# Block-causal attention and a gated feed-forward layer on one core: the constant of unseen keys is added by one-row products on PE instead of by ACT, the planner's ranks are set anew, and the last tokens' second half gets a tile of its own

## The chip, the core and the metric

The kernel runs on one core of a Trainium2 chip. The core has five engines that run side by side, each through its own list of instructions in order: the matrix engine TensorE (PE; its weight loads are listed apart as PEld), VectorE (DVE), ScalarE (ACT), GpSimd (POOL), and SyncE (SP), which here only issues DMAs. They wait for each other through semaphores. PE reads its operands from SBUF and writes to PSUM; DVE and ACT read and write both. The metric is the time of one execution in microseconds (us), as the median of several runs.

## The reference

Inputs are `q`, `k`, `v` of 8 batches, 8 heads, 576 tokens and 64 numbers a head, and three weights of a feed-forward layer. What is computed:

```python
scores = scale * np.matmul(q, k.transpose(0, 1, 3, 2))
block_i = pos[:, None] // 64
block_j = pos[None, :] // 64
scores = np.where(block_i >= block_j, scores, -1000000000.0)
scores = scores - np.max(scores, axis=-1, keepdims=True)
attn = np.exp(scores)
attn = attn / (np.sum(attn, axis=-1, keepdims=True) + 1e-09)
x = np.matmul(attn, v)          # then heads side by side: 4608 tokens of 512
g = x @ w_gate
out = (g * (1.0 / (1.0 + np.exp(-g))) * (x @ w_val)) @ w_out
```

The feed-forward layer has 512 inputs, 1536 hidden channels and 512 outputs. A query sees the keys of its own block of 64 and of earlier ones.

## The kernel before, in words

**Attention.** The heads are worked on in pairs. Scores are laid out with 128 keys (a *chunk*) on the partitions and the queries along the rows, so 576 keys make five chunks, of which a query only needs those up to its own. In a *mixed* chunk, the one that holds a query's own block, the first 64 queries must not see the last 64 keys. There the kernel adds -1e9, which the later exponential turns into 0.

Batches 0 and 1 (`plain_scores`) are split into two stretches of queries, 0 to 256 and 256 to 576 (`FIRST`). A pair's steps are: loads of q and k; PE turns them (L403) and ACT copies them out of PSUM as `parts` (L411); PE multiplies keys by queries (L429), the two heads of a pair on 64 rows of the array each; ACT copies the scores to SBUF (`sc`, L447); ACT goes over the first 64 queries of each mixed chunk again and adds the bias `unseen` (0 for 64 keys, -1e9 for 64) with L452, and for chunk 0 also writes the start of the running maximum `mx` in two pieces (L460, and L461 with the bias). In batch 0's first stretch the scores stay in PSUM: ACT adds the bias there (L470) and copies them to `mx` (L473). Then DVE takes the maximum over the chunks (L603), POOL over the 128 keys (L607), DVE subtracts it (L631), ACT takes the exponential (L635), and PE multiplies by `v`, with the two heads on 64 columns of the array each, and for batch 0 also by `ones` for the sums (L675). Batches 2 to 7 (`split_scores`, L555 and after) work on all 576 queries of two pairs at once; their products are on the full array, and their scores, masked at L575, are not part of the change.

**Feed-forward.** Tokens come in 18 tiles of 256. Each number is split into a high and a low part, and each product is three matrix products (L998 to L1000 into `gv`, L1089 to L1091 into `po` or `at`). The weights arrive in 36 pieces (`weight`), each loaded raw into a `wo` tile and then unpacked by ACT (L857, L861, L876, with a tile `ob` that POOL has filled with zeros at L274) and by DVE (L866, L871, L879). Tiles 0 and 1 are worked on while batches 0 and 1 are, and while the weights come in.

**The order.** Each step is a task with an engine, a cost, a rank and what it waits for. `in_order` runs the program on paper with these costs and gives every engine its list: of the tasks that could start, the one of lowest rank goes next. The order on each engine is then fixed. Ranks come from tables: `FIRST` for the pairs of the first two batches, `PIECES` and `AHEAD` for the weight pieces and the earlier loads of some, `SIDE` and `MIXED` for tiles 0 and 1, `LEAD` for the later batches. Costs come from `act_us`, `dve_us`, `mm_us` and `pair_us`; PE pays 0.2 where a task's `mode` differs from the one before.

**The end.** The last 128 tokens go out in two halves, the first copied from PSUM by ACT (L1116), the second by DVE (L1114), both into one tile `ob`.

Of the kernel before, what the change touches and what calls it, by code (L numbers as in the profile page):

```python
# [18 lines left out]
def kernel(  # L19
# [33 lines left out]
    LEAD, EAGER = 1.88, 0.3  # L53
# [3 lines left out]
    MIXED = (0, 0, 0, 1, 1, 0, 1, 0, 1, 0, 1, 1)  # L57
# [3 lines left out]
    AHEAD = {(0, 1): 2.01, (0, 2): 2.03, (1, 0): 2.5, (1, 1): 2.07, (1, 2): 2.07}  # L61
    LATER = 0.6

    PIECES = [
        (2.64, 2.64, 2.71),
        (2.85, 3.37, 2.76),
        (5.12, 5.12, 4.37),
        (4.66, 4.68, 4.68),
        (2.95, 3.91, 4.11),
        (4.18, 4.18, 4.91),  # L70
        (4.71, 4.38, 4.79),
        (2.20, 2.82, 2.82),
        (1.32, 1.14, 0.01),
        (1.91, 1.85, 2.33),
        (0.26, 1.61, 0.56),
        (2.08, 2.78, 1.84),
    ]

    SIDE = (3.40, 10.26)
# [4 lines left out]
        0: [(0, 256, (2.02, 2.21, 2.06, 2.08)), (256, 576, (1.99, 2.09, 0.10, 2.03))],  # L84
        1: [(0, 256, (1.33, 2.46, 3.26, 3.40)), (256, 576, (1.79, 1.87, 2.05, 2.09))],
# [76 lines left out]
    def act_us(n):  # L162
        return 0.08 + n * 0.000833
# [19 lines left out]
    ones = const.tile([P, D], F32, name="ones")  # L183
# [4 lines left out]
    nc.vector.memset(unseen[BLK:P], HIDDEN)  # L188
    seen = const.tile([P, 1], F32, name="seen")
# [144 lines left out]
    def attention(R, b, h, a, e, early, bufs, lane):  # L334
# [4 lines left out]
        Q = R - (0.001 if early else EAGER)  # L339
# [30 lines left out]
        def plain_scores():  # L370
# [21 lines left out]
            for i in range(2):  # L392
                ps = Buf("gv") if whole else Buf("at", also=banks)
                nb = len(blocks[i])
                per = nb if nb < 6 else 3

                def turned(ps=ps):
                    return ps[0].rearrange("p (x n) -> p x n", x=1) if whole else ps[0]

                def transposes(i=i, turned=turned, per=per):  # L400
                    for m, c in enumerate(blocks[i]):
                        o = m % per * TB
                        nc.tensor.transpose(  # L403
                            turned()[:, m // per, o : o + TB],
                            qk[0][:TB, lane * 3 + c, 2 * i * D : 2 * (i + 1) * D],
                            ident[:TB, :TB],
                        )

                def out_of_psum(i=i, turned=turned, nb=nb, per=per):
                    o = L + blocks[i][0] * TB  # L410
                    nc.scalar.mul(  # L411
                        prt[i][:, o : o + nb * TB].rearrange("p (x n) -> p x n", x=nb // per),
                        turned()[:, 0 : nb // per, 0 : per * TB],
                        1.0 if i else SCALE,
                    )

                tr = add("PE", 0.083 * nb, R, transposes, [ld[i]], [qk, ps, prt])
                ready.append(add("ACT", act_us(nb * TB), R, out_of_psum, [tr], [ps, prt]))

            for visit in visits:  # L420
                both = [Buf("at", also=banks) for _ in visit]

                def products(visit=visit, both=both):
                    for parts, ps in zip(visit, both):
                        o = 0
                        for c, qs, w in parts:
                            for x in range(2):
                                rows = slice(x * D, (x + 1) * D)
                                nc.tensor.matmul(  # L429
                                    ps[0][:, x, o : o + w],  # L430
                                    lhsT=prt[1][rows, L + c * P : L + (c + 1) * P],
                                    rhs=prt[0][rows, L + qs : L + qs + w],
                                    start=True,
                                    stop=True,
                                )
                            o += w

                ws = [w for parts in visit for _, _, w in parts]
                pr = add("PE", pair_us(*ws), Q, products, ready, [*both, prt, sc], mode="rows")
                for parts, ps in zip(visit, both):  # L440
                    gw = sum(w for _, _, w in parts)
                    mixed = [(c, sum(w for _, _, w in parts[:i])) for i, (c, qs, _) in enumerate(parts) if qs == c * P]
# [6 lines left out]
                    def hide(mixed=mixed, ps=ps):  # L449

                        for c, o in mixed:
                            nc.scalar.activation(  # L452
                                sc[0][:, :, place[c] : place[c] + BLK],
                                ps[0][:, :, o : o + BLK],
                                AF.Identity,
                                bias=unseen,
                            )

                    def first_max(ps=ps):
                        nc.scalar.copy(mx[0][:, :, L + BLK : L + P], ps[0][:, :, BLK:P])  # L460
                        nc.scalar.activation(  # L461
                            mx[0][:, :, L : L + BLK], ps[0][:, :, 0:BLK], AF.Identity, bias=unseen
                        )

                    if whole:
                        stays.append(ps)

                        def hide_there(ps=ps):
                            x = ps[0].rearrange("p x (n w) -> p x n w", w=2 * P)[:, :, :, 0:BLK]
                            nc.scalar.activation(x, x, AF.Identity, bias=unseen)  # L470

                        def max_there(ps=ps):
                            nc.scalar.copy(mx[0][:, :, L : L + W], ps[0][:, :, 0:W])  # L473

                        t = add("ACT", act_us(4 * BLK) + 0.1, Q, hide_there, [pr], [ps])
                        t = add("ACT", act_us(2 * W), Q, max_there, [t], [ps, mx])
# [3 lines left out]
                    t = add("ACT", act_us(2 * gw), Q, out_of_psum, [pr], [ps, sc])  # L480
                    if mixed:
                        t = add("ACT", 0.28 * len(mixed), Q, hide, [t], [ps, sc])
                    if parts[0][:2] == (0, 0):
                        t = add("ACT", 0.46, Q, first_max, [t], [ps, mx])
# [3 lines left out]
        def split_scores():  # L488
# [48 lines left out]
            for x in range(2):  # L537
                for group in (((0, 0, half), (0, half, half)), ((1, 4), (2, 3))):
# [42 lines left out]
                    t = add("ACT", act_us(2 * gw), Q, out_of_psum, [pr], [ps, sc])  # L581
# [105 lines left out]
        for i, s0, s1, _ in pieces:  # L687
# [4 lines left out]
            if s1 - s0 > here:  # L692
                ends.append(add("ACT", act_us(s1 - s0 - here), R, out_of_psum, [pr], [ps, xu]))

        if here:
# [15 lines left out]
            t = add("DVE", 1.2, 1.0, invert, [pr], [ps, sr, xt])  # L711
# [54 lines left out]
        if direct:  # L766
# [4 lines left out]
            sm = [add("ACT", act_us(W - here), R, sums_there, [pr], [ps, sr])] * 2  # L771
# [40 lines left out]
    def weight(i, kind):  # L812
# [70 lines left out]
        if wide:  # L883
            t = add("ACT", act_us(DM), R, signs, [t], [raw, y])
            f = add("DVE", dve_us(DM), R, fraction, [t], [raw, y], True)
            t = add("ACT", act_us(DM), R, scaled, [t], [raw])
            t = add("DVE", dve_us(DM), R, exponent, [t, f], [raw], True)
        t = w_high[i, kind] = add("ACT", act_us(DM), R, high, [t], bufs)
# [75 lines left out]
    def feed_forward(j, t0, w, xs):  # L964
# [50 lines left out]
        for i in range(0, NFC, 2):  # L1015
# [35 lines left out]
            a = add("ACT", act_us(n), E, tanh, [tg], [pg, t])  # L1051
# [53 lines left out]
        for m in range(nb):  # L1105
            ob = Buf("ob", "out")

            halves = 2 if ends_alone and m == nb - 1 else 1
            for x in range(halves):
                cols = slice(x * DM // halves, (x + 1) * DM // halves)  # L1110
# [11 lines left out]
                us = (dve_us if x else act_us)(DM // halves)  # L1122
# [61 lines left out]
    def in_order():  # L1184
# [17 lines left out]
        spare = {"PE": 2.0, "DVE": 0.3, "ACT": 0.3, "POOL": 0.0, "SP": 0.0}  # L1202
# [107 lines left out]
```

## Time and profile before

| | us |
|---|---|
| median of 3 runs | 1183.08 (1180.5 to 1184.99) |
| the profiled execution | 1180.03 |
| its span, first to last instruction | 1178.2 |
| PE busy | 1148.2 (97%) |
| DVE busy | 768.9 (65%) |
| ACT busy | 635.9 (54%) |
| POOL busy | 324.9 (28%) |
| 16 DMA engines, share in q1 | 56.8% |

The profile is of one execution. An engine is busy while an instruction of its own runs; waits, branches and the issuing of DMAs don't count. Matrix products overlap, so the start of one to the start of the next says more of PE's pace than the duration of one. A product of 32-bit floats (L403 aside, all products of attention in batches 0 and 1) shows as two records, one for each pass. A name like ACTq is the engine's sequencer, where DMAs are issued. In a row of waits stands who waited, for whom, the total in us, how often, and the longest. A row of groups has the line, engine, operation, tiles and shapes, the count, then the busy time and the mean in ns, then idle time before and what ended it. Buffer numbers are left out of tile names.

### The profile page before, as it was taken

What the parts mean: (1) busy time and instruction counts of PE and PEld (TensorE: products, weight loads), DVE (VectorE), ACT (ScalarE), POOL (GpSimd) and SP (SyncE); (2) the same over time, 40 slices, a digit from 0 to 9 for tenths busy, and PEclk for the clock granted to TensorE, in tenths of its full rate; (3) what the DMA queues carried; (4) which work ended last, traced back from release to release, by engine and by line L of the source; (5) the groups of instructions that cost most, each with busy time, mean ns of one, the idle gap of its engine ahead of it and who ended that gap; (6) DMA issues with size and microseconds to landing.
All of it is one profiled execution on the core that took longest, in us unless ns stands there. A gap on an engine that the chain in (4) does not pass through costs nothing.

```text
span 1178.2 us, 21734 instructions
## 1 busy us (share of the span) xinstructions
PE 1148.2 (97%) x8464; PEld 1029.9 (87%) x8464; DVE 768.9 (65%) x1234; ACT 635.9 (54%) x1150; POOL 324.9 (28%) x138
## 2 busy tenths in 40 slices
PE   6889999999999999999999999999999999999998
PEld 4667777889898989898998999898989899999997
DVE  5998988876687667877585767675767633323222
ACT  6898967757574736574655556564746312212111
POOL 3122110143634162345233325243344300000000
PEclk9999999999999999999999999999999999999999
DMA  8778656755564746755656464646662445453432
GB/s 214 188 199 214 192 180 197 208 178 160 147 169 115 210 146 176 204 164 153 181 168 182 138 192 134 198 134 190 159 199 92 153 157 183 150 167 136 144 130 103
DMA packets 266983, 197.40 MB, mean 168 GB/s; under 512 B 195264, under 2 KB 231376, under 8 KB 266880
## 3 DMA queue, kind: packets, MB, share of 16 engines
q1 hardware_dynamic: 264304, 195.29, 56.8%
q8 instruction: 66, 1.08, 0.4%
q10 hardware_dynamic: 2576, 0.72, 0.3%
q14 instruction: 37, 0.30, 0.1%
HBM read 171.57 MB, written 24.38 MB: 166 GB/s over the span
## 4 chain that ended last, share of the span: by engine, by line
PE 84%; ACT 6%; DVE 5%; DMA 2%; POOL 1%; issue 1%; SPq 0%; ACTq 0%; DVEq 0%; POOLq 0%
PE gv L998 15%; PE gv L1000 15%; PE gv L999 15%; PE po L1089 7%; PE po L1090 7%; PE po L1091 7%; PE at L555 7%; PE at L675 7%; POOL mx L607 1%; DVE mx L603 1%; DVE sc L631 1%; ACT sc L447 1%; ACT ob L857 1%; ACT sc L635 1%; DVE wo L866 1%
## 5 line engine op out<-in xcount | busy, mean ns | idle before, releaser
L607 POOL PARTITION_ALL_REDUCE mx<-mx x80 | 144.6, 1855 | 405.7 <-DVE mx L603 192.6
L998 PE MATMUL gv<-xhl,v_all 128*128 128x256 f32 x864 | 241.5, 280 | 0.7 <-DVE t L1039 0.7
L1000 PE MATMUL gv<-xhl,v_all 128*128 128x256 f32 x864 | 239.4, 277 | 0.0
L999 PE MATMUL gv<-xhl,v_all 128*128 128x256 f32 x864 | 239.3, 277 | 0.0
L726 POOL PARTITION_ALL_REDUCE mx<-mx x48 | 178.1, 3758 | 205.8 <-DVE mx L603 205.8
L1034 DVE SCALAR_TENSOR_TENSOR t<-t,gv 128x512 f32<-128x512 f32 x108 | 74.0, 685 | 209.3 <-ACT t L1031 208.9
L998 PEld LDWEIGHTS gv<-xhl,v_all 128*128 128x128 f32 x864 | 162.1, 188 | 4.9 <-issue 2.7
L999 PEld LDWEIGHTS gv<-xhl,v_all 128*128 128x128 f32 x864 | 162.3, 188 | 0.9
L1000 PEld LDWEIGHTS gv<-xhl,v_all 128*128 128x128 f32 x864 | 162.2, 188 | 0.0
L1031 ACT ACTIVATE t<-gv 128x512 f32<-128x512 f32 x108 | 64.5, 598 | 169.5 <-PE gv L1000 169.4
L1089 PE MATMUL po<-wo,hhl 128*128 128x512 f32 x372 | 147.7, 397 | 0.3 <-ACT ob L1116 0.3
L1090 PE MATMUL po<-wo,hhl 128*128 128x512 f32 x372 | 145.6, 391 | 0.0
L1091 PE MATMUL po<-wo,hhl 128*128 128x512 f32 x372 | 145.1, 390 | 0.0
L1044 ACT CAST hhl<-t 128x512 fp32r<-128x512 f32 x108 | 67.2, 622 | 139.3 <-DVE t L1039 138.0
L631 DVE TENSOR_TENSOR sc<-sc,mx 128x640 f32<-128x640 f32 (+6 forms) x168 | 123.9, 773 | 18.5 <-POOL mx L607 18.3
L635 ACT ACTIVATE sc<-sc 128x1024 f32<-128x1024 f32 (+3 forms) x104 | 105.5, 1028 | 35.8 <-DVE sc L631 35.1
L998 PE MATMUL gv<-xhl,g_even 128*128 128x256 f32 x432 | 123.2, 285 | 0.1
L999 PE MATMUL gv<-xhl,g_even 128*128 128x256 f32 x432 | 122.3, 283 | 0.2 <-DVE xhl L326 0.2
L1000 PE MATMUL gv<-xhl,g_even 128*128 128x256 f32 x432 | 122.1, 283 | 0.0
L1039 DVE SCALAR_TENSOR_TENSOR t<-t,gv 128x512 f32<-128x512 f32 x108 | 73.9, 684 | 73.1 <-PE gv L1000 72.7
L998 PE MATMUL gv<-xhl,g_odd 128*128 128x256 f32 x432 | 120.7, 279 | 0.7 <-ACT g_odd L876 0.7
L1000 PE MATMUL gv<-xhl,g_odd 128*128 128x256 f32 x432 | 119.7, 277 | 0.6 <-DVE g_odd L879 0.6
(157 smaller groups left out, 2465.2 us busy)
## 6 DMA issues: line engine op xcount, KB each, us to landing
wo<-wo_d SPq DMA_DIRECT2D x200, 512.0 KB
out_dram<-ob SPq DMA_DIRECT2D x35, 256.0 KB
v<-in_v_dram SPq DMA_DIRECT2D x64, 128.0 KB
xt<-x_d SPq DMA_DIRECT2D x64, 128.0 KB
rt<-r_d SPq DMA_DIRECT2D x128, 64.0 KB
qk<-in_q_dram SPq DMA_DIRECT2D x112, 72.0 KB
qk<-in_k_dram SPq DMA_DIRECT2D x104, 72.0 KB
x_d<-xu SPq DMA_DIRECT2D x24, 288.0 KB
```

Of the source, the lines that this page charges most:

```text
L555: nc.tensor.matmul(ps[0][:, i, o : o + w], lhsT=prt[x][1][:, c * P : (c + 1) * P], rhs=m, start=not low, stop=low == 1,)
L607: nc.gpsimd.partition_all_reduce(m, m, channels=P, reduce_op=bass_isa.ReduceOp.max)
L631: nc.vector.tensor_tensor(piece(c), scores_of(c), m, ALU.subtract)
L635: nc.scalar.activation(x, x, AF.Exp)
L675: nc.tensor.matmul(ps[0][own(x), 1 - i if sums else i, q0 - s0 : s1 - s0], lhsT=ones if sums else vt[0][:, 2 * lane + c, own(x)], rhs=sc[0 ...
L726: nc.gpsimd.partition_all_reduce(m, m, channels=P, reduce_op=bass_isa.ReduceOp.add)
L998: nc.tensor.matmul(o, lhsT=hi[:, d], rhs=xhi[:, 0:w], start=first, stop=False)
L999: nc.tensor.matmul(o, lhsT=hi[:, d], rhs=xlo[:, 0:w], start=False, stop=False)
L1000: nc.tensor.matmul(o, lhsT=lo[:, d], rhs=xhi[:, 0:w], start=False, stop=last)
L1089: nc.tensor.matmul(po, lhsT=hi, rhs=whi, start=i + y == 0, stop=False)
L1090: nc.tensor.matmul(po, lhsT=hi, rhs=wlo, start=False, stop=False)
L1091: nc.tensor.matmul(po, lhsT=lo, rhs=whi, start=False, stop=i + y == NFC - 1)
```

## The change

Four things change.

- *The constant.* A new tile `shade` has 64 columns of 0 and 64 columns of 1 (the second half now serves as `ones`), and a new tile `hidden` holds -1e9. After the products of each mixed chunk in batches 0 and 1, two more products with one row each (one for each head, from partitions 0 and 64) add `shade` times `hidden` onto the first 64 queries in PSUM. The chip's instructions name their tile of the array: 64 x 128 for the score products, 32 x 128 for the new ones. ACT's steps L452, L461 and L470 of these batches go, and L460 copies all 128 queries.
- *Costs on paper.* ACT's tasks that read PSUM cost 0.05 and the others 0.093 besides the elements (before: 0.08 for all), three steps of the weights cost more, the new products 0.117 a pair; three numbers in `spare` change.
- *Ranks.* `LEAD`, `LATER`, `MIXED`, `AHEAD`, `PIECES`, `SIDE` and `FIRST` are new. In batches 0 and 1 a task of the scores now ranks 0.3 ahead of its pair's other tasks (before: 0.001).
- *The last tokens.* The second half of the last 128 tokens goes through a `t` tile, the first through `ob`.

```diff
-    LEAD, EAGER = 1.88, 0.3
+    LEAD, EAGER = 1.79, 0.3
...
-        0: [(0, 256, (2.02, 2.21, 2.06, 2.08)), (256, 576, (1.99, 2.09, 0.10, 2.03))],
+        0: [(0, 256, (-0.54, -0.36, -5.34, -0.08)), (256, 576, (-5.88, -1.74, -1.43, -0.73))],
...
-    def act_us(n):
-        return 0.08 + n * 0.000833
+    def act_us(n, psum=False, more=0.0):
+        return (0.05 if psum else 0.093) + n * 0.000833 + more
...
-    ones = const.tile([P, D], F32, name="ones")
+    shade = const.tile([P, 2 * BLK], F32, name="shade")
+    nc.vector.memset(shade[:, 0:BLK], 0.0)
+    ones = shade[:, BLK : BLK + D]
     nc.vector.memset(ones, 1.0)
...
+    hidden = const.tile([P, 1], F32, name="hidden")
+    nc.vector.memset(hidden, HIDDEN)
...
-        Q = R - (0.001 if early else EAGER)
+        Q = R - (0.3 if early else EAGER)
...
                                     start=True,
+                                    stop=qs > c * P,
+                                )
+
+                            for x in range(2) if qs == c * P else ():
+                                nc.tensor.matmul(
+                                    ps[0][:, x, o : o + BLK],
+                                    lhsT=shade[x * D : x * D + 1, :],
+                                    rhs=hidden[x * D : x * D + 1, :].to_broadcast([1, BLK]),
+                                    start=False,
                                     stop=True,
                                 )
                             o += w
 
                 ws = [w for parts in visit for _, _, w in parts]
+                ws += [BLK for parts in visit for c, qs, _ in parts if qs == c * P]
...
-                    def hide(mixed=mixed, ps=ps):
-
-                        for c, o in mixed:
-                            nc.scalar.activation(
-                                sc[0][:, :, place[c] : place[c] + BLK],
-                                ps[0][:, :, o : o + BLK],
-                                AF.Identity,
-                                bias=unseen,
-                            )
-
                     def first_max(ps=ps):
-                        nc.scalar.copy(mx[0][:, :, L + BLK : L + P], ps[0][:, :, BLK:P])
-                        nc.scalar.activation(
-                            mx[0][:, :, L : L + BLK], ps[0][:, :, 0:BLK], AF.Identity, bias=unseen
-                        )
+                        nc.scalar.copy(mx[0][:, :, L : L + P], ps[0][:, :, 0:P])
...
-                        def hide_there(ps=ps):
-                            x = ps[0].rearrange("p x (n w) -> p x n w", w=2 * P)[:, :, :, 0:BLK]
-                            nc.scalar.activation(x, x, AF.Identity, bias=unseen)
...
-            ob = Buf("ob", "out")
...
             for x in range(halves):
+                ob = Buf("t") if x else Buf("ob", "out")
...
-        spare = {"PE": 2.0, "DVE": 0.3, "ACT": 0.3, "POOL": 0.0, "SP": 0.0}
+        spare = {"PE": 2.37, "DVE": 0.40, "ACT": 0.38, "POOL": 0.0, "SP": 0.0}
```

How the order moves, at two places. First PE, where the first feed-forward products of tile 0 (`gv`, from the gate weights `g_even`) and the scores of a pair's second stretch (`at`, `po`, from `parts`) meet. Before, from the first feed-forward product on:

```order
L998 MATMUL gv_0_138<-xhl_0_78,g_even_76 128x256
L999 MATMUL gv_0_138<-xhl_1_79,g_even_76 128x256
L1000 MATMUL gv_0_138<-xhl_0_78,g_even_77 128x256
L429 MATMUL at_0_164<-parts_0_148,parts_1_149 128x320 x2
L429 MATMUL at_0_164<-parts_0_148,parts_1_149 128x192 x2
L998 MATMUL gv_0_138<-xhl_0_80,g_even_76 128x256
L999 MATMUL gv_0_138<-xhl_1_81,g_even_76 128x256
L1000 MATMUL gv_0_138<-xhl_0_80,g_even_77 128x256
L429 MATMUL po_0_210<-parts_0_148,parts_1_149 128x320 x2
L429 MATMUL po_0_210<-parts_0_148,parts_1_149 128x64 x2
```

And the same place now, with the end of a `v` and sums product of a second stretch ahead of it:

```order
L669 MATMUL at_0_168<-sc_0_217,shade 64x64 x2
L992 MATMUL gv_0_153<-xhl_0_81,g_even_79 128x256
L993 MATMUL gv_0_153<-xhl_1_82,g_even_79 128x256
L994 MATMUL gv_0_153<-xhl_0_81,g_even_80 128x256
L434 MATMUL at_0_205<-parts_0_161,parts_1_162 128x320 x2
L434 MATMUL at_0_205<-parts_0_161,parts_1_162 128x192 x2
L443 MATMUL at_0_205<-hidden,shade 128x64 x2
L434 MATMUL po_0_219<-parts_0_161,parts_1_162 128x320 x2
L434 MATMUL po_0_219<-parts_0_161,parts_1_162 128x64 x2
L443 MATMUL po_0_219<-hidden,shade 128x64 x2
```

A pair of one-row products (L443) stands behind each mixed chunk, and the first feed-forward product is number 70 of PE's list where it was number 31: all four first stretches of batch 0, and the scores, exponentials and products of one second stretch, now go before it. Of the 40 one-row pairs 14 stand ahead of that place.

Second ACT, at the very start of the program (`qk` are the loaded keys, `seen` a small tile whose only use is to load the table of exponentials, `wo` a raw weight piece). Before:

```order
L1142 ACT_TABLE_LOAD
L1142 ACTIVATE seen<-seen 128x1
L379 DMA qk_0_124<-in_k_dram 96x3x64 x2
L379 DMA qk_0_127<-in_k_dram 96x3x64 x4
L411 ACTIVATE parts_0_148<-gv_0_138 128x288
L379 DMA qk_0_124<-in_k_dram 96x3x64 x2
L411 ACTIVATE parts_1_149<-gv_0_154 128x288
L470 ACTIVATE at_0_164<-at_0_164,unseen 128x4x64
```

And now, up to the first step of a weight:

```order
L384 DMA qk_0_126<-in_k_dram 96x3x64 x2
L384 DMA qk_0_129<-in_k_dram 96x3x64 x2
L384 DMA qk_0_126<-in_k_dram 96x3x64 x2
L384 DMA qk_0_129<-in_k_dram 96x3x64 x2
L1136 ACT_TABLE_LOAD
L1136 ACTIVATE seen<-seen 128x1
L416 ACTIVATE parts_0_161<-gv_0_153 128x288
L416 ACTIVATE parts_1_162<-gv_0_157 128x288
L470 COPY mx_0_179<-at_0_168 128x2x256
...
L470 COPY mx_0_179<-at_0_205 128x2x256
L851 ACTIVATE ob_0_231<-wo_0_97 128x512
```

All eight loads of keys stand ahead of the table load, the bias in PSUM (L470 of the kernel before) is gone, and the second pair's copy to `mx` (L470 now) stands ahead of the first weight's first step (L851 now), which it followed before.

64 lines of the change are left out of this document (30 added, 34 removed).

## The prediction

> **What bounds the kernel now.** I read the page first, then the busy time by stage, then what the matrix engine (PE) waits for in the stage that the change touches. The page gives the span and PE's share:
>
> ```profile
> span 1178.2 us, 21734 instructions
> PE 1148.2 (97%) x8464; PEld 1029.9 (87%) x8464; DVE 768.9 (65%) x1234; ACT 635.9 (54%) x1150; POOL 324.9 (28%) x138
> ```
>
> PE is idle for 30.0 us of 1178.2. The stages tell where. The columns are the stretch and its length, then the busy time of PE, PEld (weight loads), DVE, ACT and POOL with the number of instructions, the granted PE clock, the DMA share and GB/s:
>
> ```profile
> 0.00:26.00 26.00, 16.75 (x114) 12.71 (x114) 13.47 (x41) 15.53 (x31) 9.18 (x16) 0.93 0.84 209
> 26.00:60.00 34.00, 28.20 (x225) 20.40 (x222) 32.13 (x65) 30.43 (x59) 7.71 (x6) 0.95 0.74 198
> 60.00:90.00 30.00, 26.20 (x193) 19.77 (x194) 27.96 (x51) 27.49 (x57) 8.03 (x6) 0.94 0.72 195
> 90.00:120.00 30.00, 28.21 (x241) 23.58 (x240) 25.14 (x47) 26.06 (x55) 8.34 (x6) 1.00 0.79 207
> 120.00:150.00 30.00, 29.67 (x224) 23.88 (x224) 28.40 (x49) 28.21 (x51) 5.77 (x4) 1.00 0.63 185
> 150.00:180.00 30.00, 29.69 (x209) 23.14 (x208) 25.22 (x45) 18.07 (x32) 5.97 (x4) 1.00 0.57 184
> 180.00:200.00 20.00, 18.26 (x117) 14.32 (x117) 18.14 (x34) 15.43 (x26) 0.00 (x0) 1.00 0.69 207
> 240.00:1100.00 860.00, 858.21 (x6361) 787.12 (x6360) 547.26 (x827) 433.13 (x773) 274.33 (x94) 1.00 0.56 163
> ```
>
> From 240 to 1100 us PE is idle for 1.8 us of 860: new ranks have nothing to win there, and PE's work there is the same. Everything is decided in the first 200 us, where PE idles 26 - 16.75 = 9.3 us before the first feed-forward product (at 26 us), and 174 - 160.2 = 13.8 us between 26 and 200. Between 26 and 150 three engines are full at once: of 124 us PE is busy 112.3 (91%), DVE 113.6 (92%), ACT 112.2 (90%). So work that moves from ACT to PE leaves one full engine for another. The largest of PE's waits between 26 and 200 us (who waits, for whom, total, times, longest):
>
> ```profile
> PE at L403 <- ACT parts L411: 2.3, 2, 2.1
> PE at L429 <- ACT parts L411: 1.8, 1, 1.8
> PE at L675 <- ACT sc L447: 1.7, 1, 1.7
> PE at L403 <- ACT sc L452: 1.0, 1, 1.0
> PE po L403 <- ACT sc L452: 0.9, 1, 0.9
> PE gv L998 <- ACT g_odd L876: 0.7, 1, 0.7
> ```
>
> These six are 8.4 of the 13.8 us, and all end on ACT. What ACT's relief can win in this stage is therefore bounded by these 8.4 and a few smaller waits of the kind, some 10.
>
> **The change, part by part.** *ACT loses work.* The groups that go, with busy time and mean, and one copy of 128x256 as the price of what replaces the last two:
>
> ```profile
> L452 ACT ACTIVATE sc<-at,unseen 128x128 f32<-128x128 f32 x29 | 10.2, 393 | 0.0
> L452 ACT ACTIVATE sc<-po,unseen 128x128 f32<-128x128 f32 x3 | 1.2, 384 | 0.0
> L461 ACT ACTIVATE mx<-at,unseen 128x128 f32<-128x128 f32 x4 | 1.7, 433 | 0.0
> L460 ACT COPY mx<-at 128x128 f32<-128x128 f32 x4 | 1.2, 307 | 0.0
> L587 ACT COPY mx<-sc 128x256 f32<-128x256 f32 x24 | 9.7, 403 | 0.7
> ```
>
> 10.2 + 1.2 + 1.7 + 1.2 less four copies of 0.40 is 12.7 us, and the four pieces of L470 (one of 0.45 us is quoted with the start, below) make it about 14.4. That is busy time off the path: ACT is 90% busy, and it counts only as far as a PE wait goes with it.
>
> *PE gains 40 pairs of one-row products* (5 mixed chunks, 4 pairs of heads, 2 batches). The trace has no such product, so I price it from the nearest one, the pair of 64 columns that chunk 4 has. Here it stands behind a pair of 320 columns, and 1.5 us later the pair of 320 columns stands alone:
>
> ```profile
> 138.38 0.28 PE L999 MATMUL gv<-xhl,v_all 128*128 128x256 f32 x1
> 138.50 0.28 PE L1000 MATMUL gv<-xhl,v_all 128*128 128x256 f32 x1
> 138.71 0.98 PE L429 MATMUL at<-parts,parts 64*128 64x320 f32 x8
> 139.61 0.38 PE L998 MATMUL gv<-xhl,g_odd 128*128 128x256 f32 x1
> 139.84 0.28 PE L999 MATMUL gv<-xhl,g_odd 128*128 128x256 f32 x1
> 139.95 0.28 PE L1000 MATMUL gv<-xhl,g_odd 128*128 128x256 f32 x1
> 140.16 0.81 PE L429 MATMUL at<-parts,parts 64*128 64x320 f32 x4
> 140.90 0.39 PE L998 MATMUL gv<-xhl,v_all 128*128 128x256 f32 x1
> ```
>
> From start to start, 320 and 64 columns take 139.61 - 138.71 = 0.90 us, 320 alone 140.90 - 140.16 = 0.74: a pair of 64 columns costs 0.16. The same rows price the way in and out of products on half the rows: the last full product before takes 138.71 - 138.50 = 0.21 where its neighbour took 0.12, and the first after takes 139.84 - 139.61 = 0.23 where the next takes 0.11. That is 0.09 for emptying and 0.12 for a weight load that nothing covers, 0.21 for each change of shape. Every one-row pair stands behind products on 64 rows, and I count 102 changes of shape in PE's order before and, if one row is a shape of its own, 161 now.
>
> The Trainium skill, TensorEngine Tiling, Key Properties, says that changing the tiling mode drains the engine, and its list of tilings has 32 rows apart from 64. By that rule the one-row products pay the 0.21 each way; without it they would pay 0.16 alone. The trace agrees for 64 rows against 128 (0.21 a change); no run here shows 32 against 64.
>
> 14 of the 40 pairs stand ahead of the first feed-forward product, where PE idles anyway; 26 stand behind it, 10 of these followed by products on 64 rows again (two new changes), 16 by another shape (one new change, since the way out was paid before). Behind it: 26 x 0.16 = 4.2, and 36 changes x 0.21 = 7.6, together 11.7 us. Lower bound 4.2 (no price for a change); nothing below, since PE can't skip the products. I take 11.7, because each change of shape that the trace does show costs that.
>
> *PE's waits shrink.* Between 0 and the 10 us that end on ACT. L452's own 1.9 go for sure; of the rest much goes, since ACT has 14 us less to do and since what PE does longer ahead of a wait shortens it. DVE, as full as ACT, keeps its work and stays a limit. I take 8.
>
> *The start.* Rows of ACT and POOL there:
>
> ```profile
> 0.73 1.28 ACT L1142 ACT_TABLE_LOAD   x1 [0.73 <-PEq L1293]
> 1.18 0.92 ACTq L379 DMA_DIRECT2D qk<-in_k_dram  x2
> 2.13 2.45 ACTq L379 DMA_DIRECT2D qk<-in_k_dram  x4
> 4.74 0.41 ACT L411 ACTIVATE parts<-gv 128x288 f32<-128x288 f32 x1 [2.51 <-PE gv L403]
> 5.13 0.87 ACTq L379 DMA_DIRECT2D qk<-in_k_dram  x2
> 8.21 0.45 ACT L470 ACTIVATE at<-at,unseen 128x256 f32<-128x256 f32 x1 [1.75 <-PE at L429]
> 13.00 0.78 ACT L857 ACTIVATE ob<-wo 128x512 f16<-128x512 f32 x1 [1.68 <-POOL ob L274]
> 14.57 0.56 ACT L473 COPY mx<-at 128x512 f32<-128x512 f32 x1
> ```
>
> All eight K loads now stand ahead of the table load: 0.73 + 0.92 + 2.45 + 0.87 + 1.28 is 6.25, so the first L411 (line 416 now) starts 1.5 us later than 4.74, and the first scores some 0.7 later. The one-row pairs put about 0.32 + 4 x 0.21 = 1.2 into the first pair's chain and L470's 0.45 leaves it. Against that, the second pair's copy to the maxima (L473) no longer stands behind L857, which waited 1.68 for a fill on POOL; and the feed-forward now begins behind more attention. Both sides are 1 to 3 us; I take 0, bounds -2 and +4.
>
> *The end.* The last two copies went one behind the other, the second waiting for the first's tile:
>
> ```profile
> 1174.64 0.44 DVE ob L1114
> 1175.07 0.02 issue
> 1175.10 0.37 ACT ob L1116
> ```
>
> With a tile each they run together: 0.4 us less.
>
> *Sum*, against the profiled execution's own 1180.0 us (span 1178.2 and 1.8 around it): +11.7 - 8 + 0 - 0.4 = +3.3. The median of the three runs, 1183.1, is 3.0 above that execution; carried over, the forecast is 1186 us. About 0.5% (6 us) is what a measurement of this kernel can tell from no change.
>
> **The rivals.** *A, the forecast (0.45):* what PE pays about matches what it no longer waits for; within 6 us.
>
> *B, ACT was the limit (0.27).* The one-row products share the array with 64 rows and pay no change of shape: 4.2 us. With the order planned for it nearly all of the 10 us of ACT waits go, and 2 at the start. 4.2 - 10 - 2 - 0.4 = -8: about 1175. For it: every large wait of PE in this stage ends on ACT. Against it: 0.21 at each change of shape seen.
>
> *C, DVE takes ACT's place (0.28).* DVE is 92% busy from 26 to 150, and the change takes nothing off it. The pieces that ACT drops then only let ACT wait for DVE; PE's waits end on tiles that come a step later, and only L452's own 1.9 us are saved, while the one-row products cost their 11.7: +11.7 - 1.9 - 0.4 = +9.4, about 1192. It decides from the point where less than 6 of the 10 us of waits go. For it: three engines at 90%, and PE's work is what everything behind 240 us hangs on. Against it: PE's delay itself gives DVE time.
>
> Had the drain rule of TensorEngine Tiling no force between 32 and 64 rows, B would be likelier than C; by the rule it is the other way, and the trace bears it out as far as it goes.
>
> **How the numbers follow.** Chances: A 0.45, B 0.27, C 0.28. The range reaches from B with 2 us more won (1173) to C with the start's worse bound in part (1196). Faster by over 0.5% means under 1177.2: B with few exceptions, 0.25. Slower by over 0.5% means above 1189: C and a little of A's upper edge, 0.3. Between them 0.45.
>
> **What would show it right or wrong.** The 80 new products (160 records, as each of these products shows two) stand on PE in the first 200 us, with a start-to-start time of about 0.4 to 0.6 us for a pair where 64-row products follow; 0.16 to 0.2 there would mean no drain and speak for B. PE's waits for ACT between 26 and 200 should fall from 10 to about 2 us; if they stay and end on DVE, C holds. PE's idle time ahead of the first feed-forward product against 9.3 us tests the start. ACT's busy time should fall by 14 us, DVE's and POOL's stay. From 240 us to the end all should be shifted by one amount; if that stretch is longer or shorter by over 3 us, the ranks work where I gave them no effect, and the prediction's reasons are wrong even if its time holds.

## The result, and the profile after

The kernel after takes 1218.35 us (median of 4 runs, 1217.34 to 1220.39) against 1182.80 for the kernel before in the same session: a ratio of 1.0305, with a 95% interval of 1.0282 to 1.0328. It is 3% slower. The forecast was 1186 us in a range of 1173 to 1196, so time, range and the likeliest case were wrong.

The page of after, the two lines that the prediction began with:

```profile
span 1218.6 us, 22012 instructions
PE 1173.0 (96%) x8624; PEld 1045.5 (86%) x8624; DVE 772.8 (63%) x1236; ACT 629.0 (52%) x1110; POOL 324.0 (27%) x138
```

The busy time by stage of after. Columns as before: PE, PEld, DVE, ACT, POOL, then the granted PE clock, DMA share and GB/s:

```profile
0.00:26.00 26.00, 18.39 (x98) 12.97 (x100) 8.46 (x30) 10.95 (x21) 8.86 (x16) 1.00 0.68 157
26.00:200.00 174.00, 166.10 (x1303) 126.38 (x1300) 148.51 (x275) 132.08 (x225) 34.57 (x26) 0.98 0.68 187
200.00:300.00 100.00, 77.94 (x510) 68.49 (x509) 75.63 (x112) 66.45 (x119) 27.54 (x10) 0.86 0.59 162
300.00:700.00 400.00, 395.61 (x2945) 360.79 (x2945) 288.94 (x431) 228.15 (x403) 154.66 (x53) 1.00 0.59 163
```

and the two of these stretches in which before differs most, from the profile of before:

```profile
26.00:200.00 174.00, 160.24 (x1199) 125.08 (x1195) 157.01 (x286) 145.69 (x273) 35.82 (x26) 0.98 0.69 196
200.00:300.00 100.00, 98.07 (x717) 90.23 (x716) 73.22 (x112) 66.66 (x120) 31.20 (x12) 1.00 0.64 179
```

Up to 200 us PE idles less than before (26 - 18.39 + 174 - 166.10 = 15.5 us against 23.0). But from 200 to 300 us it idles 22.1 us, where it idled 1.9, its clock falls to 0.86, and it issues 510 instructions where it issued 717. An estimate that counts only work that both kernels do, each product at its pace at full clock, has PE some 10 us behind before at 200 us, 36 at 300 and 40 at the end (the two profiled executions differ by 40). Most of the loss arises from 200 to 300 us, behind the stretch in which the prediction said that everything is decided.

What PE waits for in after, first from 26 to 200 us, then from 200 to 300:

```profile
PE at L669 <- ACT sc L629: 1.7, 1, 1.7
PE at L408 <- ACT parts L416: 1.6, 2, 0.9
PE at L434 <- ACT sc L461: 1.4, 2, 1.1
```

```profile
PE gv L994 <- DVE v_all L873: 14.9, 1, 14.9
PE gv L992 <- DVE t L1033: 3.2, 2, 2.3
```

One wait of 14.9 us is new. The timeline of after there, PE first, then ACT's, POOL's and DVE's part (start, duration, idle before in brackets):

```profile
238.99 0.41 PE L993 MATMUL gv<-xhl,v_all 128*128 128x256 f32 x1
254.31 0.58 PE L994 MATMUL gv<-xhl,v_all 128*128 128x256 f32 x1 [14.91 <-DVE v_all L873]
```

```profile
228.67 0.64 ACT L870 CAST v_all<-wo 128x512 fp32r<-128x512 f32 x1
246.34 7.66 POOL L720 PARTITION_ALL_REDUCE mx<-mx  x2 [11.43 <-DVE mx L597]
246.99 2.77 DVE L597 TENSOR_TENSOR mx<-mx,sc 128x384 f32<-128x384 f32 x1
249.80 3.75 DVE L517 TENSOR_TENSOR parts<-sr,parts 64x576 fp32r<-64x576 f32 x2
253.57 0.69 DVE L873 TENSOR_TENSOR v_all<-wo,v_all 128x512 fp32r<-128x512 f32 x1
```

PE has the high part of the last value weight and stands for its low part. ACT wrote the high part at 228.67; the subtraction that makes the low one (L873) starts 24.9 us later. Its row shows no wait for another engine: it stands in DVE's list behind maxima and splits of batches 2 and 3. That is the twelfth row of `PIECES`, whose ranks the change sets to 14.60, 16.59, 15.95, where no rank of the other eleven rows of after is above 8.13. Behind the wait the clock is down:

```profile
254.30:258.10 3.80, 3.79 (x18) 0.50 0.43 139
258.10:261.50 3.40, 1.08 (x8) 1.00 0.00 0
261.50:264.90 3.40, 3.40 (x12) 0.50 0.25 77
```

Two stretches of 3.8 and 3.4 us run at half clock, each behind a stretch in which PE was mostly idle. (The clock was down shortly before the long wait too: the product at 238.99 takes 0.41 us, where one of its kind takes 0.28 in the prediction's rows.) The Trainium skill, TensorE: Matmul & The Clock Gate, its part on the HAM clock gate, says that the clock is set by how busy PE was in a window of about 3.4 us; the trace agrees with a half-clock stretch of 3.4 us. So here PE's idle time is paid for twice.

### The profile page after: what moved, and what is told of

It reads as the page before. It is cut to its first block, busy times and chain, and to the rows that moved or that the text cites. A ratio compares the mean times of both kernels' runs of the same rounds, so it can differ in the third digit from the quotient of the medians.

```text
span 1218.6 us, 22012 instructions
## 1 busy us (share of the span) xinstructions
PE 1173.0 (96%) x8624; PEld 1045.5 (86%) x8624; DVE 772.8 (63%) x1236; ACT 629.0 (52%) x1110; POOL 324.0 (27%) x138
## 4 chain that ended last, share of the span: by engine, by line
PE 80%; DVE 6%; ACT 5%; DMA 4%; issue 2%; POOL 2%; SPq 1%; DVEq 0%; ACTq 0%; POOLq 0%
PE gv L992 14%; PE gv L994 14%; PE gv L993 14%; PE at L669 7%; PE po L1083 7%; PE po L1084 7%; PE po L1085 7%; PE at L549 6%; DMA wo<-in_moe_w_out_dram 2%; DVE sc L625 1%; PE at L434 1%; ACT qk L511 1%; POOL mx L601 1%; DMA wo<-in_moe_w_val_dram 1%; DVE mx L597 1%
## 5 line engine op out<-in xcount | busy, mean ns | idle before, releaser
L994 PE MATMUL gv<-xhl,v_all 128*128 128x256 f32 x864 | 240.5, 278 | 14.9 <-DVE v_all L873 14.9
L1028 DVE SCALAR_TENSOR_TENSOR t<-t,gv 128x512 f32<-128x512 f32 x108 | 74.0, 685 | 211.5 <-ACT t L1025 211.0
L992 PE MATMUL gv<-xhl,g_odd 128*128 128x256 f32 x432 | 120.8, 280 | 0.0
L994 PE MATMUL gv<-xhl,g_odd 128*128 128x256 f32 x432 | 119.8, 277 | 0.2 <-DVE g_odd L873 0.2
L993 PE MATMUL gv<-xhl,g_odd 128*128 128x256 f32 x432 | 119.6, 277 | 0.0
```

The source lines that it names most:

```text
L992: nc.tensor.matmul(o, lhsT=hi[:, d], rhs=xhi[:, 0:w], start=first, stop=False)
L993: nc.tensor.matmul(o, lhsT=hi[:, d], rhs=xlo[:, 0:w], start=False, stop=False)
L994: nc.tensor.matmul(o, lhsT=lo[:, d], rhs=xhi[:, 0:w], start=False, stop=last)
L1028: nc.vector.scalar_tensor_tensor(t[0][:, 0:n], t[0][:, 0:n], 1.0, pg[0][:, 0:n], ALU.add, ALU.mult)
```

## The experiments

All times are medians; ratios are to the kernel before on the same chip. Up to the fifth run two theories stood against each other. R: the new ranks, since the last weight piece is unpacked behind attention of batches 2 and 3. P: the one-row products cost so much that the plan slips behind them.

**Products over 64 rows, in the order of after.** 63 of the 64 rows hold zero.

```diff
-    nc.vector.memset(hidden, HIDDEN)
+    nc.vector.memset(hidden, 0.0)
+    for x in range(2):
+        nc.vector.memset(hidden[x * D : x * D + 1], HIDDEN)
...
-                                    lhsT=shade[x * D : x * D + 1, :],
-                                    rhs=hidden[x * D : x * D + 1, :].to_broadcast([1, BLK]),
+                                    lhsT=shade[x * D : (x + 1) * D, :],
+                                    rhs=hidden[x * D : (x + 1) * D, :].to_broadcast([D, BLK]),
```

> The changed kernel with the constant added by products of 64 rows instead of one (63 of them add zero), so that they have the shape of the score products beside them; every engine's order stays as it is. Theory R (ranks): the new ranks let the last weight piece be unpacked behind the attention of batches 2 and 3, and PE's stall of 15 us at 239 us is theirs. Then the stall stays, and only the changes of shape go: 36 x 0.21 = 7.6 us behind the start and some of the 5 us before it, so 1207 to 1212 us. Theory P (price): the plan didn't know the price of the one-row products, PE runs behind it and the stall follows from that. Then most of the 35 us go with the changes of shape: under 1198 us.

1210.11 us, ratio 1.0236 (1.0217 to 1.0255). The change of shape is worth 8 us; the wait of 14.9 us stays as it was. So of what P blames, the change of shape has at most 8 of the 36 us; what the products cost besides it, this run doesn't show.

**One step of the last piece earlier, in after.** Only DVE's subtraction for the value weight.

```diff
-        t = add("DVE", dve_us(DM), R, low, [t], bufs, True)
+        t = add("DVE", dve_us(DM), 5.0 if (i, kind) == (11, 1) else R, low, [t], bufs, True)
```

> The changed kernel with one rank of one task set to 5.0 instead of 16.59: DVE's last step on the last piece of the value weights. The orders are the same up to 228 us of the changed kernel's profile. Theory R: PE's wait of 14.9 us for this step goes, with the half clock around it, 15 to 24 us in all: 1195 to 1204 us. Theory P: PE is late anyway and meets the next late step; over 1210 us.

1219.94 us, 1.0322 (1.0298 to 1.0345): nothing won. PE's waits from 200 to 300 us in this run:

```profile
PE po L1083 <- ACT wo L870: 11.9, 1, 11.9
PE gv L992 <- DVE t L1028: 4.3, 2, 3.8
PE po L1084 <- DVE wo L873: 2.1, 1, 2.1
```

The wait for `v_all` is gone; PE now stands for the same piece's output weight (`wo`), whose steps kept their late ranks. One step was too little: a piece is three weights, and the last to be ready sets the end.

**The ranks, costs and end of before with the one-row products, planned anew** (the diff of the change in `plain_scores` and the tiles `shade` and `hidden`, nothing else).

> The kernel before with the one-row products in place of ACT's pieces, with its own ranks, costs and end. Theory R: without the new ranks no stall of over 3 us behind 200 us; the products cost what the prediction gave them less the waits they end, between +3 and +11 us: 1186 to 1194 us. Theory P: the plan is as wrong about their price as in the changed kernel, 1205 us or more.

1215.97 us, 1.0296 (1.0271 to 1.0321). Without the new ranks it is nearly as slow. R as it stood falls.

**The ranks of after with ACT's pieces, planned anew** (the reverse).

> The changed kernel with ACT's pieces back and no one-row products; ranks, costs and the end are the new ones, and the plan is made anew. Theory R: the late weight piece is in the ranks, so the kernel stays slow: 1200 to 1212 us, with PE waiting over 8 us for a weight piece between 200 and 270 us. Theory P: within 8 us of the kernel before, under 1191 us.

1227.38 us, 1.0382 (1.0353 to 1.0412). Without the products it is slower still. P falls too. Both runs let the planner write the order again, and with after there are now three new orders that cost 34 to 46 us, whatever they were made for. From here on a third theory, O: the loss is in the order, and a theory can only be tested with the order held still.

**One-row products in the order of before.** Every task keeps its cost and rank, so all five lists are those of before row for row; the tasks of ACT's pieces stay in the plan and issue nothing.

> The kernel before with its order kept row for row on all five engines (same plan, same costs and ranks in the paper clock), but with the change's one-row products behind the diagonal products, and without ScalarE's 36 pieces that add the constant (the first maxima's two copies become one). It computes the full result. This is the change with its ranks, costs and end left out. Theory P (the one-row products themselves cost far more than I priced, because everything that PE holds up slips behind them): 1205 to 1220 us, and the stretch from 200 to 300 us loses over 10 us of TensorE's time. Theory O (the products cost about what the sum said, and the rest of the loss is the newly planned order): 1180 to 1194 us, by the prediction's sum without its term for the end 1186.5; TensorE's idle time from 200 to 300 us stays under 4 us, as before the change.

1196.33 us, 1.0119 (1.0096 to 1.0143). Between P and O: the products alone cost 14.6 us, four times the sum, yet well under half of the loss. The stages:

```profile
0.00:26.00 26.00, 19.29 (x98) 13.05 (x98) 8.54 (x33) 11.05 (x21) 9.20 (x16) 1.00 0.75 169
26.00:200.00 174.00, 167.02 (x1274) 130.88 (x1275) 147.92 (x271) 131.66 (x224) 33.14 (x26) 0.97 0.65 181
200.00:300.00 100.00, 94.90 (x664) 84.94 (x663) 71.17 (x115) 62.67 (x112) 23.26 (x8) 0.97 0.67 191
```

PE idles 6.7 us up to 26 and 7.0 from 26 to 200 us, 9.3 less than before in the same stretches. But PE is late by then and has done less of its list: up to one and the same product, which before issues at 200 us, it idles 16.1 us against 23.0, so 6.9 less. The profiled execution is the slowest of the six: 1199.83 us, 19.8 above the profiled one of before. Since the order is the same, each of the 40 pairs can be set against its own place in before: from the start of the last product ahead of it to the start of the next one behind it takes 20.0 us more over all pairs, 6.0 of them for the eight ahead of 30 us. These eight run at half pace, though the column of the granted clock has 1.00 there: in this run

```profile
7.15 1.23 PE L434 MATMUL at<-parts,parts 64*128 64x256 f32 x4 [1.63 <-ACT parts L416]
8.30 0.69 PE L443 MATMUL at<-hidden,shade 1*128 1x64 f32 x4
8.92 0.80 PE L434 MATMUL at<-parts,parts 64*128 64x128 f32 x4
```

the pair of 256 columns takes 1.15 us and the one-row pair behind it 0.62, where the same take 0.64 and 0.36 at 86 us (next fence).

**The same with products over 64 rows.**

> As the run in the order of before with one-row products, but each product takes 64 rows (one of them holds the constant, 63 hold zero), so that TensorE sees no change of shape between the 64-row scores, the mask and the next 64-row scores. The price of a change of shape (0.21 us by the trace of before; 36 of them in the sum) then goes: 3 to 8 us less than with one-row products. Theory O: 1177 to 1188 us, and if it comes out under 1181, a version that beats both kernels. Theory P: over 1200, since 64 rows stream as long as one row does.

1189.01 us, 1.0052 (1.0034 to 1.0069): 7.3 less than with one row, and 1 us above the 1177 to 1188 of theory O. The same three pairs in both runs, one-row first, then 64 rows:

```profile
86.19 0.70 PE L434 MATMUL at<-parts,parts 64*128 64x256 f32 x4
86.83 0.44 PE L443 MATMUL at<-hidden,shade 1*128 1x64 f32 x4
87.19 0.49 PE L434 MATMUL at<-parts,parts 64*128 64x128 f32 x4
87.61 0.44 PE L443 MATMUL at<-hidden,shade 1*128 1x64 f32 x4
87.98 0.81 PE L434 MATMUL at<-parts,parts 64*128 64x320 f32 x4
88.72 0.44 PE L443 MATMUL at<-hidden,shade 1*128 1x64 f32 x4
89.09 0.38 PE L1002 MATMUL gv<-xhl,v_all 128*128 128x256 f32 x1
```

```profile
79.75 0.70 PE L436 MATMUL at<-parts,parts 64*128 64x256 f32 x4
80.28 0.33 PE L445 MATMUL at<-hidden,shade 64*128 64x64 f32 x4
80.45 0.44 PE L436 MATMUL at<-parts,parts 64*128 64x128 f32 x4
80.73 0.34 PE L445 MATMUL at<-hidden,shade 64*128 64x64 f32 x4
80.91 0.81 PE L436 MATMUL at<-parts,parts 64*128 64x320 f32 x4
81.55 0.34 PE L445 MATMUL at<-hidden,shade 64*128 64x64 f32 x4
81.81 0.39 PE L1004 MATMUL gv<-xhl,v_all 128*128 128x256 f32 x1
```

From the first product to the feed-forward product behind the last pair it is 2.90 us with one row, 2.06 with 64. With one row the 256 columns ahead take 0.64 to the next start, with 64 rows 0.53: that is the emptying. The three pairs then take 0.36, 0.37 and 0.37 to the next start, with 64 rows 0.17, 0.18 and 0.26. The Trainium skill, TensorEngine Tiling, Key Properties, has the drain at a change of mode; here are the rows that the trace of before could not show, and they agree: one row behind 64 empties the array, 64 behind 64 do not.

**After with its twelfth piece at rank 7.0.** Order as in after up to about 225 us.

```diff
-        (14.60, 16.59, 15.95),
+        (7.00, 7.00, 7.00),
```

> The kernel after with one row of ranks changed: the twelfth piece of the weights ranks at 7.0 (in place of 14.60, 16.59 and 15.95), so that its three weights are loaded and unpacked ahead of the attention of batches 2 and 3. Up to about 225 us the order is that of after on every engine, then it differs. It computes the full result. If the late last piece makes the loss of 200 to 300 us (26 us of 36 there): 1190 to 1200 us, and no wait of PE for a weight over 3 us. If what counts is that the whole new order runs late from its first weights on, and the last piece is only the place where that shows: 1208 to 1222 us, with other waits in 200 to 300 us.

1194.18 us, 1.0099 (1.0075 to 1.0123): 24 us less than after. From 200 to 300 us, and the two low parts that PE had stood for:

```profile
200.00:300.00 100.00, 96.24 (x689) 86.47 (x686) 76.39 (x122) 67.27 (x124) 26.33 (x10) 1.00 0.70 198
```

```profile
225.20 0.68 DVE L873 TENSOR_TENSOR v_all<-wo,v_all 128x512 fp32r<-128x512 f32 x1
233.08 0.69 DVE L873 TENSOR_TENSOR wo<-wo,wo 128x512 fp32r<-128x512 f32 x1
```

`v_all` is ready at 225.9 us in place of 254.3, the output weight at 233.8; PE idles 3.8 us there in place of 22.1, at full clock. One row of ranks is 24 of the 36 us.

**That row alone, in before** (the twelfth row becomes 14.60, 16.59, 15.95).

> The kernel before with one row of ranks changed: the twelfth piece of the weights gets the ranks that the change gives it (14.60, 16.59, 15.95 in place of 2.08, 2.78, 1.84), behind the attention of batches 2 and 3. Up to TensorE's row 735, ScalarE's 290 and VectorE's 311 the order is that of before, then it differs. It computes the full result. This is that row of the change done alone. If the late last piece makes the loss at 200 to 300 us by itself: 1197 to 1212 us (15 to 30 us more than before), TensorE idle for over 8 us between 190 and 280 us with a wait for a weight over 5 us, and a half clock behind it. If it hurts only where the whole start runs late (one-row products in front): 1180 to 1190 us.

1187.22 us, 1.0037 (1.0025 to 1.0049): the first expectation missed, 4 to 5 us and no more. The last piece is unpacked at 215.5 us where before has it at 211.9. A rank only says who goes first among steps that could start. In the order of before the eleven other pieces are early (the 24th weight is unpacked at 141.9 us, in after at 156.5), and in this run none of the maxima and splits of batches 2 and 3 stands among DVE's last steps for the piece (206 to 215.5 us); in after they do. So the row does its harm only together with the rest of the new order. That the late start of that order is what makes the difference fits, but no run tried it alone.

**The order of after without its products.** Row for row after, but ACT adds the constant again, in before's pieces, right behind the copies.

> The order of after row for row on all five engines (its ranks, its plan, its late twelfth piece), but without the 40 pairs of one-row products: ScalarE adds the constant again, in the pieces of before, each right behind the copy that it belonged to. It computes the full result. It completes a square: order of before with ScalarE's pieces (the kernel before), with one-row products (14.6 us more), order of after with one-row products (35.5 more), and this one. If the new order loses by itself (the late piece): 1203 to 1212 us, with a wait of TensorE over 8 us for a weight between 220 and 270 us. If the order loses only because the products make its start run late: 1180 to 1195 us, with no such wait.

1217.76 us, 1.0294 (1.0271 to 1.0316), 6 us slower than the first expectation allowed, with the wait that it named. Its stretch and its wait:

```profile
200.00:300.00 100.00, 78.15 (x508) 68.28 (x507) 75.55 (x113) 65.55 (x118) 27.52 (x10) 0.86 0.59 162
```

```profile
PE gv L999 <- DVE v_all L878: 14.9, 1, 14.9
```

The same wait, the same clock, the same time as after, and no one-row product in it. The new order loses by itself; the products are not needed for it.

**The same with the twelfth piece at 7.0.**

> The same (order planned for one-row products, ScalarE's pieces in their place) with the twelfth piece of the weights at rank 7.0. It computes the full result. With one-row products this order took 1194.2 us, 2 us less than one-row products in the order of before. If products and order add: 1178 to 1183 us, so a version at the time of before or 2 us under it. If this order needs ScalarE free of the pieces (it was planned so): 1186 to 1196 us.

1189.00 us, 1.0051 (1.0034 to 1.0068); products and order do not simply add, the second expectation holds. Without the late piece the new order still costs 6.7 us more than that of before with the same pieces on ACT.

**After with both mended** (64 rows and rank 7.0).

> The kernel after with the twelfth piece of the weights at rank 7.0 and the products that add the constant over 64 rows (63 of them zero), both of which gave time back alone. It computes the full result. If the two losses are separate and add up: 1194.2 less the 7.3 us that 64 rows gave back in the order of before, so 1185 to 1189 us. If one hides the other (the 64 rows make TensorE reach the weights earlier and wait there): 1191 to 1196 us.

1185.61 us, 1.0031 (1.0019 to 1.0044): the two losses add up (8.6 us less than with one row). So the late piece is 24 of the 36 us, the shape 8.6, and 3.4 are left. In this order one-row products (1194.2) lose to ACT's pieces (1189.0) by 5.2 us. Products over 64 rows have a median 3.4 us under that of the pieces; the two intervals of the ratio overlap (1.0019 to 1.0044, 1.0034 to 1.0068), so this gain is likely and not sure.

**64 rows for 16 of the 40 pairs, in the order of before**: a counter lets the ninth to the 24th diagonal tile have a product, the others ACT's piece.

> The order of before row for row, and its pieces of ScalarE for the first 8 and the last 16 of the 40 diagonal tiles; only the 16 in between, issued from about 30 to 100 us, where most of TensorE's waits for ScalarE ended, get their constant from a product over 64 rows. It computes the full result. In the run with all 40 over 64 rows the products before 30 us cost 2.9 us of TensorE's time and those behind 100 us 3.0, and the waits fell by 1.8 and 0.2 us there; between, they cost 3.7 and the waits fell by 5.5. If these terms add: 1178 to 1184 us, no change that can be measured or a gain of 2 to 3 us against before. If the loss of 5 us behind 200 us, which all runs with products on TensorE show, comes with these 16 as well: 1184 to 1189 us.

1185.86 us, 1.0028 (1.0014 to 1.0043): the terms do not add, nothing is won. At 100 us PE is level with before; from 120 to 200 us it is busy for 73.44 of 80 us where before has 77.62:

```profile
120.00:200.00 80.00, 73.44 (x520) 58.42 (x519) 68.02 (x117) 58.68 (x100) 11.14 (x8) 0.99 0.60 185
```

It waits there for ACT (2.1 us on `g_odd`, 1.9 on an exponential), though ACT has 16 pieces less in its list. The second expectation has the time right; the loss that it puts behind 200 us lies ahead of it. No version came out under the kernel before.

## Why the prediction was wrong, point by point

**The step that failed** is the sentence that from 240 to 1100 us "new ranks have nothing to win there" and that "everything is decided in the first 200 us". It read a full PE as one that new ranks can't change. That bounds what they can win; it says nothing of what they can lose. The stretch from 200 to 300 us was full because every weight was ready in time, and the diff's own table says that the last row's ranks go from about 2 to about 15, behind batches 2 and 3. The price in the order of after is 24 us (one-row products) or 29 (ACT's pieces). The prediction's last paragraph had named this as what would sink it. No rival carried it: B and C differ in what ends PE's waits for ACT, and both lie in the first 200 us. With the row set to 7.0 and the shape mended, after is 3.4 us above before.

**The price of a pair** was nearly right. Predicted: 0.16 in the stream, 0.21 for a change, so 0.37 where another shape follows and 0.58 where 64 rows follow. Measured in the order of before at full clock: 0.37 and 0.46, with 64 rows 0.17 to 0.22. One change more costs 0.2 as predicted, two cost 0.29 and not 0.42. The drain between 1 and 64 rows is there, so rival B's condition fails; it is worth 7 to 9 us in three orders (8.2, 7.3 and 8.6), where the sum had 36 x 0.21 = 7.6. That these agree so well is partly luck: the sum has two changes too dear and leaves out the pairs ahead of the first feed-forward product.

**PE's waits** shrank, but by less than the 8 of the sum. In the order of before, from the first feed-forward product to the product that before issues at 200 us, PE's idle time fell by 5.1 us (13.76 to 8.62). By the prediction's own sign its waits for ACT from 26 to 200 us should have fallen from 10 to about 2; they fell from 10.5 to 6.6, and to 7.7 in after. In after's order the pieces cost PE 19.4 us of idle time from 26 to 200 us (174 - 154.57 in the run without products), the products leave 7.9.

**The start at 0** is the second step that failed: "14 of the 40 pairs stand ahead of the first feed-forward product, where PE idles anyway". In the order of before eight of them do. The last `v` products of the first stretch and the first feed-forward product, in before and then with one-row products:

```profile
24.70 0.87 PE L675 MATMUL po<-sc,v 128*64 128x256 f32 x8
26.16 0.39 PE L998 MATMUL gv<-xhl,g_even 128*128 128x256 f32 x1
```

```profile
32.53 1.50 PE L679 MATMUL po<-sc,v 128*64 128x256 f32 x8
34.76 0.39 PE L1002 MATMUL gv<-xhl,g_even 128*128 128x256 f32 x1
```

It starts 8.6 us later, where the worse bound was 4. The eight pairs are 6.0 of it, PE's waits up to there are 1.8 us shorter, and the other 4.4 is pace: the same eight records take 0.87 us in before and 1.50 here. With 64 rows it starts at 31.21, 5.1 us later. Why full pace comes later with these products isn't shown. That PE idles for a third of a stretch does not make new work free there: the pair stands between the scores and the copy that PE waits for next. In after's own order the first scores start at 8.14 us where before has them at 6.51, 1.6 later, where the forecast had 0.7.

For the profiled execution in the order of before these terms close: 8.6 for the start, 13.9 for the 32 pairs behind it (the sum had 11.7 for 26), 5.1 less of waits (a new one of 2.2 for `g_odd` counted in), and 2.1 over the products that before issues from 200 to 240 us, where PE now waits 2.3 us for a weight's DMA (1.5 in before) and its clock is down again (0.97 from 200 to 300 us, 1.00 in before). That is 19.5 of its 19.8 us; the sum had 3.7 without its term for the end.

**ACT's busy time** fell by 6.9 us in place of 14.4. I multiplied durations, and neighbours on ACT overlap: in before three pieces from 104.69 to the next start at 105.45 take 0.25 each, not 0.39.

**The end's 0.4** did not come. In after, the two halves go to two tiles, and the second still waits:

```profile
1215.00 0.42 DVE L1108 COPY t<-at 128x256 f32<-128x256 f32 x1 [3.39 <-PE at L1085]
1215.46 0.37 ACT L1110 COPY ob<-at 128x256 f32<-128x256 f32 x1 [1.23 <-DVE t L1108]
```

ACT stands for the same 1.23 us as before. So it wasn't `ob` that it waited for; both still read the one PSUM tile `at`, but whether this is the cause wasn't tried.

**Rival C** has the sign and not the mechanism: in after PE's waits up to 200 us still end on ACT, not on DVE.

**What stays open:** why the two orders that were planned anew for a mixture (ranks of before with products, ranks of after with ACT's pieces) lose 34 and 46 us. The first has no wait of PE over 3.0 us from 180 us on, and runs at a mean clock of 0.92 from 26 to 150 us; the second waits 12.2 us for ACT's `xhl` between 300 and 700 us. Each is another order; no run took them apart.

## What to carry to other kernels

A stage in which the bound engine is full shows that its inputs come in time; ask of each step that a change moves later whether it feeds that stage, and by when. Where a planner writes the order, compare kernels with the order held still before you blame an operation: here the same edit cost 14.6 us in the order of before and 0.6 in that of after (5.2 there once the twelfth piece ranked at 7.0), and one row of ranks cost 24 to 29 us in one and 4 to 5 in the other. And an extra product pays less for its data than for the shape that it brings: 64 rows, 63 of them zero, were cheaper than one row.

## What the runs showed of the hardware

A DVE step with two operands in SBUF can take several times as long while POOL reduces over the partitions; the steps with one operand in PSUM that were compared with it don't. The groups of two DVE steps of after on 128x512, shortest, median and longest in ns:

```profile
L1041 DVE TENSOR_TENSOR hhl<-t,hhl x108: 649/692/3022, 86.9 to 1210.9; 128x512 fp32r<-128x512 f32 x108
L1028 DVE SCALAR_TENSOR_TENSOR t<-t,gv x108: 671/687/690, 69.2 to 1207.5; 128x512 f32<-128x512 f32 x108
```

L1041 reads two SBUF tiles. Where no POOL instruction overlaps it (81 of 108), it never takes more than 694 ns; the 27 others reach 3022. L1028 reads one SBUF tile and one in PSUM; 36 of its 108 overlap POOL, and none takes more than 690. The Trainium skill, SBUF — State Buffer, the section on SBUF's two separate sides, says that the two engines share a port pair that one holds for a whole instruction, against DVE instructions with two SBUF inputs; the trace agrees. In the 14.9 us wait above it is about 4.5 us, an estimate from these rows: L597 took 2.77 where the same shape takes 0.55 alone, and the pair of L517 3.75 where one takes 0.75.
